# A new order for the steps of a pooled attention and feed-forward kernel, with new buffer lists

## The chip, the cores and the metric

One Trainium2 chip, one core. The metric is device time in microseconds (us); the times are medians of a few runs of the same program.

## What is computed

Attention over pooled keys and values, and a feed-forward layer whose hidden value is the largest of three products. The reference, cut to what matters:

```python
# q, k, v: (8, 8, 576, 64): batch, heads, sequence, head size
k_p = k.reshape(B, H, Sp, 8, D).mean(axis=3)      # Sp = 72
v_p = v.reshape(B, H, Sp, 8, D).mean(axis=3)
scores = (1.0 / np.sqrt(D)) * np.matmul(q, k_p.transpose(0, 1, 3, 2))
attn = np.exp(scores - scores.max(-1, keepdims=True))
attn = attn / (attn.sum(-1, keepdims=True) + 1e-09)
a = np.matmul(attn, v_p)
x = a.transpose(0, 2, 1, 3).reshape(4608, 512)
h = np.maximum(np.maximum(x @ w1, x @ w2), x @ w3)   # 512 -> 768
out = h @ w_out                                      # 768 -> 512
```

## The kernel before

**Two pipelines that run interleaved.** The attention goes by batch `b` (0 to 7, 576 tokens each), the feed-forward layer by token block `n` (0 to 8, 512 tokens each). Each engine works through its own instructions strictly in order; the order in which the Python code emits them is fixed by hand (`manual_schedule`), from two long lists of step names, `MIDDLE` and `ORDER`. A step is one piece of work with a part on TensorE (PE) and, mostly, an evacuation of its PSUM result on ScalarE (ACT) or VectorE (DVE). A name that ends in `-` emits the PE part alone, the same name with `+` later emits the evacuation, and a bare name emits both. Since every engine has its own queue, only the order within each engine counts; a `+` and a `-` of different engines that swap places in the list change nothing.

**Steps of the attention**, written `b:step` in `MIDDLE`, and without the colon for batches 6 and 7 in `ORDER`:

- `k` transposes the pooled keys (PE) and four copies put them into `kz` (ACT, DVE). The pooled keys come from GpSimd (POOL): `k5+2` are two of the four additions that fold `k` of batch 5 (lines 190 to 194), `v5+2` the same for the values; `k5<`, `v5<`, `q5<` issue the loads on POOL's queue. Such a load waits for the newest hidden product in the list and for the newest `T`.
- `T` is one DMA transpose of the whole `q` of a batch, on SyncE's (SP) queue (line 379).
- `s0`, `s3`, `s6` are the scores of three, three and two heads (line 256). Each takes both of the two `att` tiles in PSUM; ACT empties them with 4, 4 and 2 exponentials (line 261). In the second list the scores of batch 7 come in nine flat pieces.
- `v0` to `v4` multiply the exponentials with the values for 128 tokens (line 332, one `att` tile each); DVE takes the reciprocal and normalizes into `xn` (lines 340, 342).
- `x0` to `x4` bring `xn` into the transposed ring `xT`, from batch 3 on by a DMA transpose on SP's queue (line 317).

**Steps of the feed-forward layer**, written `n/step`. For `n` up to 5 the weights have `w1` subtracted, so that two products are enough:

- `h`, twelve per block: four matmuls of 512 columns into a `pw` tile (three in all, line 450); ACT writes the rectified first product (line 456), DVE the maximum with the second into `hT` (line 458).
- `a1` to `a4` and `b1` to `b4`: DVE differences of `xT` and of `hT` (line 686), which the output needs because it is computed with seven products in place of eight. They go into `tt`.
- `1` to `7`: those products, ten matmuls of 256 columns each (line 787). `1`, `6`, `5`, `3` build on one PSUM tile, so each waits until ACT has copied the one before (line 798); `2`, `4` and the later of `5` and `7` are added by DVE (line 801). Complete rows are stored by SP (line 736).
- `f` and `S`: DVE sums of weights for later blocks. `!` makes the next fold on POOL wait for the newest of the DVE steps `a`, `b`, `f`, `S`.

In `ORDER` blocks 6 to 8 get their hidden layer by seven products as well (`1a` to `7c`, line 864), `o1` to `o7` are the output products of blocks 5 and 7, `F` is a part of the output of block 6 (lines 498, 502), and `T` without a batch stands for the sums of `xT` that a block's products need.

**Buffers.** `SLOTS` says for each tile of a pool, in order of allocation, which buffer it takes. A tile's first write waits until the last user of the buffer's earlier tile is done.

The lists from which this section's steps are taken are in the function below.

Of the kernel before, what the change touches and what calls it, by code (L numbers as in the profile page):

```python
# [28 lines left out]
def kernel(  # L29
# [15 lines left out]
    B, H, S, D = q.shape  # L45
# [17 lines left out]
    PSUM = bass.MemoryType.PSUM  # L63

    SLOTS = """
        ps0.att:0120212012012 sb3.xn:0123450123450123450123450123450123540125
        psp.pw:012012012021021021021201201201201201202102010210120121021021
        psp.pw:02120120120120120101012010210210202012012012
        psp.att:010101010101010101010101010101101010101010101010101010101010
        psp.att:1010101001010101 sb3.osb:01201021021201 psq.sc:010110101010101010110101  # L70
        psq.pa:0101010100101
    """
    seats = {}
    for name in SLOTS.split():
# [5 lines left out]
    sb3 = Turns(ctx.enter_context(tc.tile_pool(name="sb3", bufs=1)), "sb3", seats, 3)  # L80
# [808 lines left out]
    def pool_step(name):  # L889
# [21 lines left out]
            held.clear()  # L911

    ORDER = """
        2a- 1a- b1 b3 1a+ o1 k7- 1b- 2a+ b2 o2- k7+ o6- v62- T 6a- o6+ s70- o5- vpool 1b+ s71- b4
        s70+ v62+ v63- 6a+ 5a- x62 s72- 7a- o2+ o5+ v63+ s71+ 6b- s73- 7a+ v64- 5a+ s75- 3a- s74-
        s72+ 4a- s73+ s75+ 6b+ s77- v64+ o3- s78- s74+ 4a+ x64 o7 s76- 2b- 1c- 2c- s77+ 2b+ 3a+
        s78+ s76+ v70- 5b- o4- x63 1c+ v70+ 2c+ 5b+ 3b- 6c- v71- x70 o4+ 3b+ 7b v71+ 1a- 6c+ 5c
        4b- o3+ 2a- 4b+ v72- 3c- v72+ F 7c- 1b- v73- T 2b- 1a+ 2a+ x71 7c+ 2c- v73+ 6a- 3c+ 1b+ 4c
        v74- 6b- 6a+ 2b+ x72 x73 5a F 3a- 7a- 2b- F 6b+ 7a+ 5b- v74+ 3a+ x74 1c 4a 5b+ F 7b- 6c-
        7b+ 2c+ 3b- F 4b- 2a- 6c+ 3b+ 1a- 5c- 4b+ 7c- 1a+ 5c+ F 7c+ 2a+ 3c- T 6a- 4c 1b- 3c+ 2c-  # L920
        6a+ 1b+ H 5a 6b- 7a- 6b+ 3a- o1- h 1c- 7a+ 5b- 3a+ 4a- o2- o1+ 1c+ 7b- 2b+ 5b+ o6- 4a+ 7b+
        6c- 4b- 2c+ o6+ o7- 6c+ 5c- 4b+ 7c- 5c+ o5- 7c+ 3c- o5+ o2+ 3b- o7+ 4c- o3- 3c+ o4- 3b+
        4c+ o3+ o4+
    """

    def weave():
# [40 lines left out]
        1/h 2:s0- 2:s0+ 2:s0+ 2:q2 1/h- 2:s0+ 1/h- 2:s0+ 1/h+ 1/b1 S 2:q3 1/h+ 1/h- S S 3:T S 1/h+  # L967
        1/a3 2:s3- 1/a1 2:s3+ 2:s3+ 1/h- 2:s3+ 1/h- 1/h+ 1/h+ 1/a2 1/h- 2:s3+ 1/a4 2:s6- 2:s6+
        1/1- 2:s6+ 1/h+ 1/b3 1/b2 1/b4 2:v0 1/2- 1/1+ 1/6- 2:v1 2:x0 1/7- 2:v2- 1/6+ 2:x1 1/5-
        1/2+ 1/7+ 2:v2+ ! k3+4 2:v3- v3+2 2:v3+ 1/5+ 2:x2 2:v4 1/3- 1/4- 2:x3 1/3+ 1/4+ 2:x4 2/h  # L970
        k5< 3:k- 2/h- 3:k+ 2/h+ 2/a1 2/a3 2/h- 2/a2 f 2/a4 f ! v3+2 v5< 2/h+ f 3:s0- 3:s0+ 3:s0+
        3:s0+ 2/h- 2/h- 2/h- 2/h+ 2/h+ 3:s0+ 2/h- 2/h+ 3:s3- 2/h+ 2/h- f 3:s3+ 2/h- 3:s3+ 2/h+
        2/h- 3:s3+ 2/b1 3:s3+ 3:s6- 2/h+ 3:s6+ 2/h- 2/h+ 2/h- 3:s6+ ! k4+2 2/h+ 2/h+ 2/b2 2/b3
        2/b4 ! k4+2 2/1- 4:T 3:v0- 2/1+ 3:v1- 3:v0+ 3:x0 2/2- 3:v1+ 2/6- 3:v2- 2/7- 3:x1 2/2+ 2/7+
        v4+2 2/6+ 3:v2+ 2/5- 3:v3- 2/5+ 3:v3+ 3:x2 3:x3 3:v4 4:k 3:x4 2/3- 2/4 2/3+ q5< 3/a3 k6<
        3/h 3/a1 3/h- 3/h- 3/h+ 3/a2 4:s0- f 3/a4 ! v4+2 4:s0+ 4:s0+ f 3/h- 3/h+ 4:s0+ 3/h+ 4:s0+
        3/h- 3/h- 3/h+ 3/h+ 4:s3- 3/h- v6< 3/h+ 3/h 4:s3+ 4:s3+ 4:s3+ 4:s3+ 3/h- 3/b1 3/h- 3/h+
        3/h+ 4:s6- 4:s6+ ! k5+2 3/h 3/h- 4:s6+ 3/1- 3/h+ 3/b2 3/b3 3/b4 3/1+ ! k5+2 v5+2 4:v0-
        3/2- 4:v0+ 4:x0 4:v1 3/6- 3/2+ 4:x1 3/6+ 3/7- 5:T 3/7+ 4:v2- 3/5- 4:v2+ ! 3/5+ 5:k- 4:v3-
        4:v4- 4:v3+ 5:k+ 4/h- 4:v4+ q6< 4/a1 4/h+ 3/3- 4/h- 4/h- 3/4- 4/a2 4/h+ 4:x2 4/h- 5:s0-  # L980
        k7< 4/a3 v5+1 f v5+1 3/4+ 4/h+ f 5:s0+ 4/h- 4:x3 4/h+ 4/h- 4/h- 5:s0+ 4:x4 5:s0+ 5:s0+
        4/h+ 4/h- 4/a4 4/h+ 5:s3- 6:T 4/h- 4/h- ! 3/3+ 4/h- 4/h+ k6+1 5:s3+ 4/h+ 4/h+ 5:s3+ 4/b1
        5:s3+ k6+1 5:s3+ 4/h+ 4/h+ 4/h 5:s6- 5:s6+ 4/b2 5:s6+ ! 4/1- 4/2- k6+1 4/b3 5:v0- k6+1
        5:v0+ 5:x0 v6+1 q7< 4/1+ 4/2+ 4/6- v6+1 5:v1- 4/6+ 5:v1+ 5:x1 4/7- 5:v2- 4/7+ 5:v2+ 4/5-
        v7< 4/b4 5:v3- 6:k- 5:v4- 4/5+ 5:v4+ 4/3- 5:v3+ 5/a3 5/h- 5/a1 6:k+ 5/h- 5:x2 6:s0- 5/h+
        6:s0+ 6:s0+ 4/4- 6:s0+ 5/h- 6:s0+ 5/h+ 6:s3- 5/h- 4/3+ 5/h- 6:s3+ 4/4+ 5:x3 5/h- 6:s6-
        5/h- ! 5/h+ 6:s3+ 5/h- 6:s3+ v6+2 k7+1 5/h+ 6:s3+ 5/a2 5/h+ 5/h- 5/h+ 6:s6+ 5/a4 5/h+
        6:s6+ 5/h- 5/h+ 5/h+ 6:v0- 5/h+ k7+1 6:v1- 5:x4 6:v0+ 6:x0 5/h- k7+1 5/h- k7+1 7:T 6:v1+
        6:x1 5/h+ 5/h+
    """  # L990
    folds = iter([f for wi in range(1, 3) for f in [fold_w(wi)] * 4])

# [85 lines left out]
```

## Time and profile before

| | |
|---|---|
| runs | 224.08, 226.4, 224.12 us; median 224.12 us |
| profiled execution | 224.31 us, of which the span of the core is 222.6 us |
| PE busy | 212.2 us (95%), 1885 matmuls |
| PE weight loads | 147.2 us (66%) |
| DVE, POOL, ACT busy | 164.0 (74%), 141.0 (63%), 122.6 us (55%) |
| granted TensorE clock | 0.997 |
| DMA | 33.55 MB, 151 GB/s in the mean |

The span runs from the first to the last instruction of the core; what lies around it is 1.7 us in this execution. PE is the engine that is almost always busy, so the time is read from PE's idle stretches and from what ended each; idle time of the other engines counts only where PE waits for them.

### The profile page before, as it was taken

What the parts mean: (1) busy time and instruction counts of PE and PEld (TensorE: products, weight loads), DVE (VectorE), ACT (ScalarE), POOL (GpSimd) and SP (SyncE); (2) the same over time, 40 slices, a digit from 0 to 9 for tenths busy, and PEclk for the clock granted to TensorE, in tenths of its full rate; (3) what the DMA queues carried; (4) which work ended last, traced back from release to release, by engine and by line L of the source; (5) the groups of instructions that cost most, each with busy time, mean ns of one, the idle gap of its engine ahead of it and who ended that gap; (6) DMA issues with size and microseconds to landing.
All of it is one profiled execution on the core that took longest, in us unless ns stands there. A gap on an engine that the chain in (4) does not pass through costs nothing.

```text
span 222.6 us, 4865 instructions
## 1 busy us (share of the span) xinstructions
PE 212.2 (95%) x1885; PEld 147.2 (66%) x1885; DVE 164.0 (74%) x308; ACT 122.6 (55%) x239; POOL 141.0 (63%) x121
## 2 busy tenths in 40 slices
PE   7798999989999999999997999999999999999992
PEld 2477744448649734974594549645899777788882
DVE  3658989037899695966487987767988988797940
ACT  2267534845784478265725673784695544553440
POOL 7974300999985969696767588995193724682020
PEclk9999999999999999999999999999999999999998
DMA  6999999989879599739986999997641574100365
GB/s 176 211 197 197 207 208 208 206 154 223 160 140 196 92 160 241 131 71 157 281 133 131 177 176 214 153 216 127 147 38 33 107 171 90 46 21 3 78 193 157
DMA packets 47303, 33.55 MB, mean 151 GB/s; under 512 B 26992, under 2 KB 42288, under 8 KB 47280
## 3 DMA queue, kind: packets, MB, share of 16 engines
q0 software_dynamic: 16944, 16.98, 47.9%
q1 hardware_dynamic: 29888, 15.87, 31.7%
q10 hardware_dynamic: 448, 0.39, 0.7%
q8 instruction: 15, 0.25, 0.4%
q14 instruction: 8, 0.07, 0.1%
HBM read 34.60 MB, written 9.44 MB: 198 GB/s over the span
## 4 chain that ended last, share of the span: by engine, by line
PE 88%; DVE 4%; DMA 3%; issue 1%; ACT 1%; SPq 0%; ACTq 0%
PE pw L450 27%; PE oA L787 14%; PE pA L864 7%; PE oC L787 7%; PE po L502 5%; PE psc L256 4%; PE pav L332 4%; PE pC L864 4%; PE oB L787 3%; PE po L498 3%; DMA ktTrue<-in_k_dram 3%; PE pm L437 2%; PE pB L864 2%; PE pqt L222 2%; PE pxt L323 2%; DVE xn L342 1%
## 5 line engine op out<-in xcount | busy, mean ns | idle before, releaser
L450 PE MATMUL pw<-xT,mw 128*128 128x512 f16 (+1 forms) x336 | 68.5, 349 | 1.7 <-issue 1.5
L450 PEld LDWEIGHTS <-mw 128*128 128x128 f16 x336 | 30.8, 98 | 27.3 <-issue 3.2
L190 POOL TENSOR_TENSOR half<-vt 72x1024 f32<-72x1024 f16 (+1 forms) x12 | 29.4, 2463 | 20.9 <-DMA vt<-in_v_dram 13.7
L261 ACT ACTIVATE et<-psc 72x512 f16<-72x512 f32 (+2 forms) x66 | 34.0, 572 | 11.1 <-PE psc L256 11.0
L458 DVE TENSOR_TENSOR hT<-t,pw 128x512 f16<-128x512 f16 (+1 forms) x42 | 25.3, 607 | 15.9 <-PE pw L450 11.0
L192 POOL TENSOR_TENSOR half<-half 72x1024 f32<-72x1024 f32 (+1 forms) x13 | 28.2, 2169 | 9.3 <-DVE tt L686 3.5
L456 ACT ACTIVATE t<-pw 128x512 f16<-128x512 f32 (+1 forms) x42 | 22.6, 538 | 17.2 <-PE pw L450 16.8
L342 DVE TENSOR_TENSOR xn<-pav,rcp 128x512 f16<-128x512 f32 x40 | 27.6, 691 | 1.4
L190 POOL TENSOR_TENSOR half<-ktFalse 96x768 f32<-96x768 f16 (+1 forms) x11 | 19.8, 1813 | 4.5 <-issue 4.3
L873 ACT CAST pad<-pA 128x512 f16<-128x512 f32 x27 | 15.5, 587 | 11.4 <-PE pA L864 11.4
L787 PEld LDWEIGHTS <-tt 128*128 128x128 f16 x200 | 18.9, 98 | 2.6 <-issue 0.2
L798 ACT COPY osb<-oA 128x512 f32<-128x512 f32 x20 | 11.8, 588 | 15.3 <-PE oA L787 15.0
L332 PE MATMUL pav<-vp,et 72*128 72x65 f16 x320 | 16.2, 194 | 0.8 <-ACT osb L507 0.7
L332 PEld LDWEIGHTS <-et 72*128 72x128 f16 x320 | 14.8, 98 | 2.5 <-issue 1.1
L841 DVE TENSOR_TENSOR pad<-pad,pC 128x512 f16<-128x512 f16 x18 | 12.3, 683 | 4.7 <-PE pC L864 3.3
L256 PEld LDWEIGHTS <-kz 64*128 64x128 bf16 (+1 forms) x161 | 8.9, 95 | 10.0 <-issue 7.4
L864 PEld LDWEIGHTS <-sw 128*128 128x128 f16 x144 | 13.6, 98 | 2.8 <-issue 0.2
L844 DVE SCALAR_TENSOR_TENSOR hT<-pad 128x512 f16<-128x512 f16 x18 | 14.5, 816 | 0.9 <-ACT pad L877 0.6
L340 DVE RECIPROCAL rcp<-pav 128x8 f32<-128x8 f32 x40 | 8.1, 202 | 9.2 <-PE pav L332 9.0
L256 PE MATMUL psc<-qT,kz 64*128 64x256 bf16 (+5 forms) x138 | 13.2, 263 | 0.8 <-DVE qT L224 0.6
L787 PEld LDWEIGHTS <-hT 128*128 128x128 f16 x126 | 12.3, 98 | 1.4
L638 POOL TENSOR_TENSOR pad<-xT 128x256 f16<-128x256 f16 x8 | 5.3, 667 | 12.3 <-DMA xT<-xn 12.3
(122 smaller groups left out, 406.4 us busy)
## 6 DMA issues: line engine op xcount, KB each, us to landing
out_dram<-osb SPq DMA_DIRECT2D x32, 128.0 KB, 4.4
ktFalse<-in_k_dram POOLq DMA_DIRECT2D x7, 576.0 KB, 8.0
qb<-in_q_dram POOLq DMA_DIRECT2D x7, 576.0 KB, 7.7
vt<-in_v_dram POOLq DMA_DIRECT2D x7, 576.0 KB, 10.6
out_dram<-osb SPq DMA_DIRECT2D x11, 256.0 KB, 5.6
mw<-in_moe_w_dram POOLq DMA_DIRECT2D x9, 256.0 KB, 9.2
ktTrue<-in_k_dram SPq DMA_DIRECT2D x3, 384.0 KB, 5.2
out_dram<-ob SPq DMA_DIRECT2D x8, 128.0 KB, 2.9
```

The lines of the kernel that those rows point to most:

```text
L190: yield e.tensor_tensor(out=f[:, at], in0=t[:, at, 0:4, :], in1=t[:, at, 4:8, :], op=ALU.add)
L192: yield e.tensor_tensor(out=f[:, :, 0:2, :], in0=f[:, :, 0:2, :], in1=f[:, :, 2:4, :], op=ALU.add)
L256: nc.tensor.matmul(out, kz_all[b % 2][f % 2][rows, h, :], qTs[b][rows, n + i0:n + i1, 64 * (h % 2):64 * (h % 2) + 64], start=True, stop=True)
L261: nc.scalar.activation(out=out, in_=in_, func=FT.Exp, scale=1.0 / 64.0)
L332: nc.tensor.matmul(pav[:, h // 4, 65 * (h % 4):65 * (h % 4) + 65], ets[b][:, h, c0:c0 + 128], vp_all[:, b, h, :], start=True, stop=True)
L342: nc.vector.tensor_tensor(out=xn, in0=pv[:, :, :, 0:D], in1=rcp.to_broadcast([128, 2, 4, D]), op=ALU.mult)
L450: mm = nc.tensor.matmul(pw, w_sb[wi][:, kc, bass.ts(jc, 128)], x[:, kc], start=(kc == 0), stop=(kc == KCH - 1))
L456: yield lambda t=t, pw=pw: nc.scalar.activation(out=t, in_=pw, func=FT.Relu)
L458: yield lambda t=t, pw=pw: nc.vector.tensor_tensor(out=hT[:, jc, c0:c1], in0=t, in1=pw, op=ALU.max)
L787: nc.tensor.matmul(p, left, right, stop=(r == 4), skip_group_check=True, start=(i in FIRST and r == 0 and (m == 0 or n == LAST)))
L864: mm = nc.tensor.matmul(p[:, w], a[:, kc, bass.ts(g, 128)], b[:, kc, :], start=(i in FIRST and w + kc == 0), stop=(w + kc == 2), skip_grou ...
L873: nc.scalar.copy(out=kept(i, g), in_=p)
```

## The change

`MIDDLE` keeps its first 170 steps, up to the middle of the seven output products of block 1 (about 73 us into the span), and gets a new order behind them; `ORDER` is new from the start. The steps are the same ones and as many. The entries of `SLOTS` change with the order of allocation, and the entry of `psq.sc` moves to the end. No function changes. Of the diff, the parts that the text speaks of (the rest of both lists is new in the same way):

```diff
-        psp.pw:02120120120120120101012010210210202012012012
+        psp.pw:01212121021021021010101021021021010101012012
...
-        1/2+ 1/7+ 2:v2+ ! k3+4 2:v3- v3+2 2:v3+ 1/5+ 2:x2 2:v4 1/3- 1/4- 2:x3 1/3+ 1/4+ 2:x4 2/h
-        k5< 3:k- 2/h- 3:k+ 2/h+ 2/a1 2/a3 2/h- 2/a2 f 2/a4 f ! v3+2 v5< 2/h+ f 3:s0- 3:s0+ 3:s0+
...
-        3/h- 3/h- 3/h+ 3/h+ 4:s3- 3/h- v6< 3/h+ 3/h 4:s3+ 4:s3+ 4:s3+ 4:s3+ 3/h- 3/b1 3/h- 3/h+
-        3/h+ 4:s6- 4:s6+ ! k5+2 3/h 3/h- 4:s6+ 3/1- 3/h+ 3/b2 3/b3 3/b4 3/1+ ! k5+2 v5+2 4:v0-
-        3/2- 4:v0+ 4:x0 4:v1 3/6- 3/2+ 4:x1 3/6+ 3/7- 5:T 3/7+ 4:v2- 3/5- 4:v2+ ! 3/5+ 5:k- 4:v3-
-        4:v4- 4:v3+ 5:k+ 4/h- 4:v4+ q6< 4/a1 4/h+ 3/3- 4/h- 4/h- 3/4- 4/a2 4/h+ 4:x2 4/h- 5:s0-
...
+        1/2+ 1/7+ ! 2:v2+ 1/5+ 2:v3 k3+1 2:v4- k3+2 2:x2 1/3- k3+1 1/4- v3+1 3:k- v3+1 2:v4+ 2/h-
+        1/3+ 3:k+ 1/4+ 2:x4 2/h- 2/h+ 2/h- 2/h+ f 2/a1 2/a3 f 3:s0- 2/a2 2/h- f k5< ! 2/h- v5<
...
+        4:s0+ 3/h- 3/h+ 4:s0+ 2/4+ 3/h- f 4:s0+ 3/h- ! 3/h- 3/h+ v4+2 4:s0+ ! 3/h+ 3/h+ 4:s3-
+        4:s3+ 4:s3+ 4:s3+ 3/a2 3/h- 3/h+ 3/h+ k5+1 4:s3+ v6< 3/a3 3/h- 3/h- 3/h+ 3/h- 3/h+ 3/h+
+        3/b1 4:s6- 4:s6+ 3/b3 3/a4 4:s6+ 3/1- 3/b2 4:v0 4:v1 3/2- 3/1+ k5+1 3/6- ! 4:v2- 3/7- 4:x1
+        3/b4 k5+2 3/2+ v5+1 3/6+ 3/5- 4:x0 4:v3- 3/7+ 4:v2+ 3/5+ 4:v3+ 4:v4- 5:k- 5:T 4:v4+ 5:k+
+        v5+1 3/3- q6< f 4/a3 4/a1 3/4- 4/h- 4/h- 5:s0- k7< 4/h- 4/h+ ! 5:s0+ 4/h- v5+1 4/h- 5:s3-
...
+        k6+1 5:s6+ 4/1- 5:s6+ 5:v0- 4/h+ 4:x4 4/b2 5:v1- 4/2- k6+1 5:v0+ ! 4/b3 k6+1 6:T 4/1+ 4/6-
+        k6+1 5:v1+ 4/7- 4/b4 5:v2- 5:x0 4/2+ 4/6+ 4/7+ 5:v2+ 4/5- 5:x1 6:k- 4/5+ v6+1 5:v3- v6+1
+        q7< 5:v4- 5:v3+ 5:v4+ 6:k+ v7< 4/3- 5/a1 4/4- 6:s0- 5/a2 6:s0+ 5/h- 5/a3 6:s0+ 5:x2 5/h-
...
+        6:v0+ 5/h+ 5/h- 5:x4 6:x0 6:v1+ 5/a4 k7+2 5/h+ 5/h- 5/h- 7:T 5/h+ 6:x1 5/h+ k7+1
```

More of the change, by code (lines that the diff above doesn't have):

```diff
@@ L65 @@
     SLOTS = """
-        ps0.att:0120212012012 sb3.xn:0123450123450123450123450123450123540125
-        psp.pw:012012012021021021021201201201201201202102010210120121021021
-        psp.pw:02120120120120120101012010210210202012012012
-        psp.att:010101010101010101010101010101101010101010101010101010101010
-        psp.att:1010101001010101 sb3.osb:01201021021201 psq.sc:010110101010101010110101
-        psq.pa:0101010100101
+        ps0.att:0120212012012 sb3.xn:0123450123450123450213450231450231450231
+        psp.pw:012012012021021021021201201201201201202102010210120212012012
+        psp.pw:01212121021021021010101021021021010101012012
+        psp.att:010101010101010101010101010101101010101010110101010101010101
+        psp.att:0101010101010101 sb3.osb:01201020120120 psq.pa:0101010100101
+        psq.sc:010101101011011011001010
     """
@@ L913 @@
     ORDER = """
[L914 to L923, printed above, removed]
+        1a- b1 1a+ b3 1b- 2a- 1b+ o1- 2a+ k7- o1+ o2- b2 o6- k7+ T 6a- o6+ 6a+ v62- vpool o2+ s70-
+        o5- s70+ s71- s72- 6b- 5a- 7a- v62+ o5+ s72+ x62 s75- b4 s71+ v63- 7a+ 5a+ s75+ s73- 3a-
+        6b+ s73+ s74- 4a- s74+ 5b- v64- 5b+ s77- s76- v63+ o7- 4a+ s76+ x63 v64+ s78- 3b- o7+ 2c-
+        1c- s77+ 3a+ 2b- s78+ v70- o4- v70+ 1c+ x64 2b+ x70 6c- o4+ o3- 2c+ 7b- 3b+ 7b+ 6c+ v71-
+        o3+ v71+ 1a- 5c- 4b T F 1a+ v72- 5c+ x71 3c- 2a- 2c- v72+ 2a+ 7c- v73- 7c+ 1b- x72 2b- 6a-
+        4c- v73+ 3c+ 1b+ 6b- v74- 6a+ 5a- x73 5a+ 4c+ F 2b+ 3a- 7a- 2b- 6b+ F v74+ 7a+ 1c- 4a- 3a+
+        4a+ 1c+ 5b- x74 5b+ F 6c- 7b- 3b- 6c+ 7b+ 3b+ F 4b- F 5c- 2c+ 1a- 7c- 5c+ T 3c- 4b+ 2a-
+        1a+ 7c+ 2a+ 6a- 4c- 1b- 3c+ 6a+ 5a- 2c- 7a- 4c+ 5a+ 3a- 7a+ H o1- 1b+ 3a+ 1c- 4a- 6b- 1c+
+        6b+ o2- 4a+ 5b- 7b- 6c- h 2b+ o1+ 5b+ o6- 7b+ 2c+ 6c+ 5c- 4b- o7- 4b+ o6+ o2+ 5c+ 7c- o5-
+        7c+ 3c- o5+ o7+ 3c+ 4c- 3b o3- 4c+ o4 o3+
     """
@@ L969 @@
         1/1- 2:s6+ 1/h+ 1/b3 1/b2 1/b4 2:v0 1/2- 1/1+ 1/6- 2:v1 2:x0 1/7- 2:v2- 1/6+ 2:x1 1/5-
-        1/2+ 1/7+ 2:v2+ ! k3+4 2:v3- v3+2 2:v3+ 1/5+ 2:x2 2:v4 1/3- 1/4- 2:x3 1/3+ 1/4+ 2:x4 2/h
-        k5< 3:k- 2/h- 3:k+ 2/h+ 2/a1 2/a3 2/h- 2/a2 f 2/a4 f ! v3+2 v5< 2/h+ f 3:s0- 3:s0+ 3:s0+
-        3:s0+ 2/h- 2/h- 2/h- 2/h+ 2/h+ 3:s0+ 2/h- 2/h+ 3:s3- 2/h+ 2/h- f 3:s3+ 2/h- 3:s3+ 2/h+
-        2/h- 3:s3+ 2/b1 3:s3+ 3:s6- 2/h+ 3:s6+ 2/h- 2/h+ 2/h- 3:s6+ ! k4+2 2/h+ 2/h+ 2/b2 2/b3
-        2/b4 ! k4+2 2/1- 4:T 3:v0- 2/1+ 3:v1- 3:v0+ 3:x0 2/2- 3:v1+ 2/6- 3:v2- 2/7- 3:x1 2/2+ 2/7+
@@ L975 @@
-        v4+2 2/6+ 3:v2+ 2/5- 3:v3- 2/5+ 3:v3+ 3:x2 3:x3 3:v4 4:k 3:x4 2/3- 2/4 2/3+ q5< 3/a3 k6<
-        3/h 3/a1 3/h- 3/h- 3/h+ 3/a2 4:s0- f 3/a4 ! v4+2 4:s0+ 4:s0+ f 3/h- 3/h+ 4:s0+ 3/h+ 4:s0+
-        3/h- 3/h- 3/h+ 3/h+ 4:s3- 3/h- v6< 3/h+ 3/h 4:s3+ 4:s3+ 4:s3+ 4:s3+ 3/h- 3/b1 3/h- 3/h+
-        3/h+ 4:s6- 4:s6+ ! k5+2 3/h 3/h- 4:s6+ 3/1- 3/h+ 3/b2 3/b3 3/b4 3/1+ ! k5+2 v5+2 4:v0-
-        3/2- 4:v0+ 4:x0 4:v1 3/6- 3/2+ 4:x1 3/6+ 3/7- 5:T 3/7+ 4:v2- 3/5- 4:v2+ ! 3/5+ 5:k- 4:v3-
-        4:v4- 4:v3+ 5:k+ 4/h- 4:v4+ q6< 4/a1 4/h+ 3/3- 4/h- 4/h- 3/4- 4/a2 4/h+ 4:x2 4/h- 5:s0-
@@ L981 @@
[L981 to L986, printed above, removed]
@@ L987 @@
-        5/h- ! 5/h+ 6:s3+ 5/h- 6:s3+ v6+2 k7+1 5/h+ 6:s3+ 5/a2 5/h+ 5/h- 5/h+ 6:s6+ 5/a4 5/h+
-        6:s6+ 5/h- 5/h+ 5/h+ 6:v0- 5/h+ k7+1 6:v1- 5:x4 6:v0+ 6:x0 5/h- k7+1 5/h- k7+1 7:T 6:v1+
-        6:x1 5/h+ 5/h+
+        1/2+ 1/7+ ! 2:v2+ 1/5+ 2:v3 k3+1 2:v4- k3+2 2:x2 1/3- k3+1 1/4- v3+1 3:k- v3+1 2:v4+ 2/h-
+        1/3+ 3:k+ 1/4+ 2:x4 2/h- 2/h+ 2/h- 2/h+ f 2/a1 2/a3 f 3:s0- 2/a2 2/h- f k5< ! 2/h- v5<
+        2/h- 3:s3- 2/h- 2/h+ v3+1 2/h- 3:s0+ 2/a4 2/h- v3+1 3:s0+ 3:s6- 2/h+ 3:s0+ ! 3:s0+ 2/h+
@@ new lines @@
+        2/h+ 3:s3+ f 3:s3+ 2/h+ 2/h+ 2/h- 3:s3+ k4+1 3:s3+ 3:s6+ 2/b1 3:s6+ 2/h- 4:T 2/h+ 3:v0-
+        2/h+ 2/h+ 3:v1- 2/h- 2/1- 2/h+ 3:v0+ 2/2- 2/1+ 3:x0 k4+1 2/b2 ! k4+1 2:x3 2/6- 2/b3 3:v1+
+        3:v2 2/2+ 2/7- k4+1 2/6+ v4+1 2/5- v4+1 3:v3- 3:x1 3:x2 2/b4 4:k- q5< k6< 3:v3+ 3:x3 3:v4-
+        2/7+ 2/5+ 3:v4+ 2/3- 3/h- 4:k+ 3:x4 3/h- 4:s0- 3/h- 3/h+ 3/h- 2/3+ 3/h+ 3/h+ 2/4- 3/a1
+        4:s0+ 3/h- 3/h+ 4:s0+ 2/4+ 3/h- f 4:s0+ 3/h- ! 3/h- 3/h+ v4+2 4:s0+ ! 3/h+ 3/h+ 4:s3-
+        4:s3+ 4:s3+ 4:s3+ 3/a2 3/h- 3/h+ 3/h+ k5+1 4:s3+ v6< 3/a3 3/h- 3/h- 3/h+ 3/h- 3/h+ 3/h+
@@ new lines @@
+        3/b1 4:s6- 4:s6+ 3/b3 3/a4 4:s6+ 3/1- 3/b2 4:v0 4:v1 3/2- 3/1+ k5+1 3/6- ! 4:v2- 3/7- 4:x1
+        3/b4 k5+2 3/2+ v5+1 3/6+ 3/5- 4:x0 4:v3- 3/7+ 4:v2+ 3/5+ 4:v3+ 4:v4- 5:k- 5:T 4:v4+ 5:k+
+        v5+1 3/3- q6< f 4/a3 4/a1 3/4- 4/h- 4/h- 5:s0- k7< 4/h- 4/h+ ! 5:s0+ 4/h- v5+1 4/h- 5:s3-
+        5:s0+ 4/h+ 4/h+ 5:s0+ v5+1 4/h- 5:s0+ 4:x2 4/h+ 4/h+ 5:s3+ f 4/h- 3/4+ 5:s3+ 4/h- 5:s3+
+        4/h- 4/h+ 4/a2 f ! 4/h- 4/h- 4/h+ 5:s3+ 3/3+ 4/a4 4/h+ 4/h+ 4/h- 4/b1 4:x3 4/h+ 4/h+ 5:s6-
+        k6+1 5:s6+ 4/1- 5:s6+ 5:v0- 4/h+ 4:x4 4/b2 5:v1- 4/2- k6+1 5:v0+ ! 4/b3 k6+1 6:T 4/1+ 4/6-
@@ L990 @@
+        k6+1 5:v1+ 4/7- 4/b4 5:v2- 5:x0 4/2+ 4/6+ 4/7+ 5:v2+ 4/5- 5:x1 6:k- 4/5+ v6+1 5:v3- v6+1
+        q7< 5:v4- 5:v3+ 5:v4+ 6:k+ v7< 4/3- 5/a1 4/4- 6:s0- 5/a2 6:s0+ 5/h- 5/a3 6:s0+ 5:x2 5/h-
+        5/h- 5/h+ 6:s0+ 6:s0+ 5/h+ 5/h+ 6:s3- 5/h- 5/h- ! 5/h+ 5/h- 6:s3+ 6:s3+ 6:s3+ 6:s3+ v6+1
+        5/h+ 6:s6- 5/h- 5/h- v6+1 5:x3 5/h+ 4/4+ k7+1 6:s6+ 6:s6+ 5/h- 4/3+ 6:v0- 6:v1- 5/h+ 5/h+
+        6:v0+ 5/h+ 5/h- 5:x4 6:x0 6:v1+ 5/a4 k7+2 5/h+ 5/h- 5/h- 7:T 5/h+ 6:x1 5/h+ k7+1
     """
```

## The prediction

> **What bounds the kernel now.** First the page, for the engines and the chain that ended last.
>
> ```profile
> PE 212.2 (95%) x1885; PEld 147.2 (66%) x1885; DVE 164.0 (74%) x308; ACT 122.6 (55%) x239; POOL 141.0 (63%) x121
> PE 88%; DVE 4%; DMA 3%; issue 1%; ACT 1%; SPq 0%; ACTq 0%
> ```
>
> PE is busy 95% of the span, and 88% of the chain is PE's own work. Then the stretch that the new order touches, from 74 us to the end of the second list at 209 us (columns: length, then busy time of each engine with its instructions), and PE's waits in it.
>
> ```profile
> 74.00:209.00 135.00, 133.30 (x1168) 94.18 (x1166) 106.93 (x188) 77.95 (x152) 90.34 (x71) 1.00 0.67 127
> ...
> PE pw L450 <- issue: 1.5, 1, 1.5
> PE psc L256 <- ACT kz L242: 0.2, 1, 0.2
> ```
>
> In these 135 us PE is idle for 1.70 us. The same work is issued in any order, so a better order can give back little more than that. 1% of the time, 2.2 us, is about what a measurement of this kernel can tell from no change. What the order can take away has no such limit. Almost all of the idle time is one wait. Last the timeline around it, on PE and on SP's queue (start, length).
>
> ```profile
> 116.64 0.68 PE L332 MATMUL pav<-vp,et 72*128 72x65 f16 x16
> 118.81 1.02 PE L450 MATMUL pw<-xT,mw 128*128 128x512 f16 x4 [1.49 <-issue]
> ```
>
> ```profile
> 113.62 1.21 SPq L317 DMA_TRANSPOSE xT<-xn  x1
> 114.94 1.21 SPq L317 DMA_TRANSPOSE xT<-xn  x1
> 116.25 2.92 SPq L379 DMA_TRANSPOSE qT<-qb  x1
> ```
>
> From issue to landing, for the second of these alone, for all 27 of line 317, and for the `T` of 116.25:
>
> ```profile
> DMA to landing us min/median/max: 3.8/3.8/3.8
> ...
> DMA to landing us min/median/max: 2.3/2.5/7.2
> ...
> DMA to landing us min/median/max: 4.9/4.9/4.9
> ```
>
> The wait is the first `4/h`. It reads the tokens of `4:x1`, issued at 114.94; that one lands after 3.8 us, at 118.7, where the median of all 27 is 2.5. Right behind it SP issues `5:T`, which lands after 4.9 (the lowest of the five `T` is 4.0).
>
> **What the change does to it.** PE's list is the same steps; I price each place where the new neighbours make PE wait, or stop making it wait. Prices of PE steps are the spacing of their starts: `h` 0.86, an output product 1.09, `v` 0.26, `s0`/`s3` 0.49, `s6` 0.38, `k` 0.13.
>
> (1) *The wait at 117.3 goes*: −1.49. Behind `4:v1` PE had 4.2 us of work before `4/h`, and the first `4/h` came ahead of `3/3`. Now `3/2`, `3/3` and `3/4` lie between as well. Bounds: −1.49, and 0 if the transposes come later by as much (5).
>
> (2) *`3:s0` no longer waits for the key copies*: −0.33. Its first score matmul starts 0.47 us ahead of the second, for 0.13 us of columns (320 at the rate of four `h` matmuls of 512 in 0.86): 0.33 lost, 0.15 of it idle. `3:k` moves ahead of the first `2/h`: three `h` and a transpose, 2.8 us, lie between it and `3:s0`, where the copies need 1.0 once ACT is free. Bounds −0.33 and 0.
>
> (3) *`4:v0` and `5:v0` come too soon behind the scores*: +0.34. They read the last exponentials of `s6`:
>
> ```profile
> 87.28 1.18 ACT L261 ACTIVATE et<-psc 72x512 f16<-72x512 f32 x2 [0.59 <-PE psc L256]
> ```
>
> `s6` starts at 86.86, the exponentials end at 88.46: 1.60 us. Before, two `h` or a second product lay between; now `s6` 0.38 and one product 1.09, together 1.47. With 0.04 of signalling, 0.17 each. Bounds 0 and 0.7 (an `h` copy of 0.6 ahead of them on ACT).
>
> (4) *`3/6` waits for `3/b2` on DVE*: +0.70. Let the last `3/h` end at 0. PE: `s6` 0.38, `3/1` 1.47, wait of (3) to 1.64, `v0` and `v1` 2.16, `3/2` 3.25, then `3/6`, which needs `b2`. DVE, by the spacing in the block before (0.45 to 0.48 behind each other): maximum at 0.27, `b1` 0.99, `b3` 1.47, `a4` 1.95, `b2` 2.3 to 2.85: in time, if nothing holds it. But a DVE step with both inputs in SBUF that meets a fold on POOL stands until the fold ends:
>
> ```profile
> 125.45 2.67 DVE L686 TENSOR_TENSOR tt<-xT,tt 128x512 f16<-128x512 f16 x1
> 129.37 2.02 DVE L686 TENSOR_TENSOR tt<-hT 128x768 f16<-128x768 f16 x1
> ...
> 125.46 2.37 POOL L192 TENSOR_TENSOR half<-half 72x1024 f32<-72x1024 f32 x1
> 129.33 3.55 POOL L190 TENSOR_TENSOR half<-ktFalse 96x768 f32<-96x768 f16 x2
> ```
>
> These took 2.67 and 2.02 us where their medians are 0.42 and 0.55, ending 0.3 and 0.4 behind the fold (127.83; the first of the two folds of the last line at 130.97). In the new list the third fold of `v4` is gated by an `f` some 1.5 us behind `2/4`, which ends at −7.4 (eight `h`, one score step). From −5.9 POOL does folds of 2.5, 1.3 and 1.6 and the issue of `v6`, 0.9: its next fold, 1.63 long, runs from 0.4 to 2.05. `b1`, wanted at 0.99, starts at 2.05; `b2` ends at 3.9; `3/6` starts at 3.95 in place of 3.25. Bounds 0 (POOL 1.1 us earlier or later) and 1.6 (the whole fold).
>
> (5) *`5:T` is late for `5:s0`*: +1.0. Behind (4), `4:v1`'s `xn` ends at 5.6. SP issues `4:x1`, `4:x0`, `5:T` 1.3 apart: 5.6, 6.9, 8.2. PE: `3/6` 3.95, `v2` 5.04, `3/7` 5.30, `3/5` 6.39, `v3`, `v4`, `5:k` to 8.1, `3/3` 8.15, `3/4` 9.24, `4/h` 10.33, `5:s0` 12.06. `x0` lands at 9.4 to 10.7, `T` at 12.2 (by 4.0) to 13.1 (by 4.9). PE waits 0.1 to 1.0 in all. I take 1.0: two `x` and a `T` in a row are just what landed in 4.9 before. The ends are 0.1 and 1.0; with a load in flight an `x` took up to 7.2, which is in a rival below.
>
> (6) *`6:s0` follows `4/4` directly*: +0.25. It needs the `att` tile that `5:v4` leaves. From the end of `4/5`: the copy and the addition end at 1.27, two pairs of reciprocal and normalization (0.84, then 0.93) at 3.05; PE has `k`, two `v`, and from 0.67 on `4/3` and `4/4`: 2.85. Before, two `h` stood there too. Bounds 0 and 2 (`b4` of block 4, in the same queue, behind a fold of 2.1).
>
> *At nothing:* the rest of both lists. `6:x0` and `7:T`: from `6:v0` to the first score of batch 7 PE has 8.5 us (it had 7.7), the way over `xn`, `x0` and `T` took 7.1 (152.60 to 159.68). Without that cover each us is one of PE. The load of `v5` now follows `k5` at once, 5 us earlier, beside the stores of block 1 and `4:T` on the other queue; `4:T` is hidden by some 17 us of PE work up to `4:s0`, but `3:x0` to `3:x2` queue behind it, with 2.8 us between the last of them and `3/h` (the 3.3 of before, 94.92 to 98.23, less `2/4`, plus an addition that now follows on DVE); it needs 2.5. `v6` goes 2 us later behind a fold, and is wanted 20 us later. The second list changes neighbours by a product or two, and each product's copy is 0.59 against products of 0.44 to 1.09 behind it, as before.
>
> Sum: −1.49 − 0.33 + 0.34 + 0.70 + 1.0 + 0.25 = +0.47 us. On the profiled execution's 224.31 that is 224.8; it lies 0.19 above the median of the runs, 224.12, so I say **224.6 us**: no change that can be measured.
>
> **A rule beside the row of (4).** The Trainium skill (SBUF — State Buffer, "Who interferes with whom") says that a DVE instruction with two SBUF inputs and a GpSimd instruction that reads SBUF exclude each other for the whole instruction, and that whoever starts first holds the ports. The two rows above agree. If the ports were shared instead, `b1` would be slowed in part and (4) would be near 0; by the rule the price is what is left of the fold. By the same rule the new order, which spreads these DVE steps between the folds, could lose more than I sum, and that is the second rival.
>
> **Rivals.**
> *The gain stays.* POOL misses `b1` and `T` lands in 4.0: (4) is 0, and from (5) at most 0.1 to 0.3 is left. −1.82 + 0.34 + 0.25 + 0.2 = −1.03: 223.1. For it: 2.3 to 2.5 is the usual landing, and the meeting of (4) hangs on 1 us. Against it: the list does put `T` behind two `x`. If (3) and (6) vanish too: 222.3, hardly 1%.
>
> *DVE falls behind between the folds: slower.* Place: blocks 2 to 4. Before, the `b` steps of a block stand together ahead of a gated fold; the new list has `2/b4`, `3/a2`, `3/a3`, `3/b1`, `4/b4` alone among maxima and normalizations while POOL folds. Price: the rest of a fold, 0.76, 2.25 and 1.47 us in three rows before, mean 1.5. The rows are 1.31, 2.67 and 2.02 us in place of 0.55, 0.42 and 0.55. They reached PE nowhere, because DVE (107 us busy of 135) had slack behind them. It decides from the point where the delay is larger than the PE work up to the next use of the `pw` or `att` tile, about 2 `h`, 1.7 us: two meetings in one block. Two more meetings that reach PE: 224.6 + 3.0 = 227.6; one: 226.1. For it: five places against three. Against it: half of the meetings fall where nothing waits.
>
> *The transposes run into the loads: slower.* `x` landed after 6 to 7.2 us four times, each with a load in flight. If `3:x2` or `4:x0` meets one, `3/h` or `4/h` waits some 3 us: 227.6; if `T` alone, 1 to 2: 226.
>
> **How the numbers follow.** The forecast 0.50 (224.6, own range 223.6 to 225.8), the gain stays 0.21 (222.3 to 223.6), DVE behind the folds 0.20 (225.8 to 228), transposes in the loads 0.09 (225.5 to 228). Faster by over 1% (below 221.9): 0.03, the end of the second case with the small waits of 0.15 to 0.2 us behind copies gone as well. Slower by over 1% (above 226.4): three quarters of the third, two thirds of the fourth and 0.03 of the first: 0.24. The rest, 0.73, lies between. The range is 222.6 to 227.2: it cuts half of the last two cases' upper parts and the tip of the second.
>
> **What would show it.** Right: the 1.5 us ahead of the first `4/h` gone; 0.2 ahead of `4:v0` and `5:v0`; `3/6` behind a `b2` that ends late, its `b1` over 1 us long; `5:s0` started by the landing of `5:T`. PE idle from 74 us to the end of the second list between 1.5 and 3 us. Wrong: several DVE rows of line 686 above 1.5 us with PE waiting for `pw` or `att`; an `x` that lands after 5 us or more right ahead of an `h`; or PE idle below 0.8 us.

## The result and the profile after

The changed kernel takes **240.5 us** in the median (239.1 to 245.3), the kernel before on the same chip 224.5; the ratio is 1.067 [1.058, 1.077]. The forecast was 224.6 with a range up to 227.2. The profiled execution takes 239.1 us, its span is 237.3. Some executions of a kernel show a lower granted clock and take longer; the ratios leave these out.

The page's rows for the engines and for the chain that ended last:

```profile
PE 213.6 (90%) x1885; PEld 147.4 (62%) x1885; DVE 160.9 (68%) x308; ACT 123.2 (52%) x239; POOL 141.9 (60%) x121
PE 65%; DMA 18%; POOL 7%; DVE 3%; SPq 3%; issue 2%; POOLq 0%; DVEq 0%
```

PE does the same work (213.6 us busy, 212.2 before), but it is 90% of the span in place of 95%, and DMA now holds 18% of the chain, 3% before. That share says little by itself: e11 below has 16% of it without the loss. The stretch from 74 us to the end of the second list, now near 224 us, cut in four (length, then busy time of PE, PEld, DVE, ACT, POOL with instructions, granted clock, DMA share, GB/s), and PE's waits in it:

```profile
74.00:90.00 16.00, 16.00 (x121) 8.82 (x119) 13.18 (x25) 10.23 (x21) 13.94 (x10) 1.00 1.12 141
90.00:112.00 22.00, 8.89 (x87) 6.62 (x85) 6.60 (x14) 4.33 (x9) 8.99 (x7) 0.74 1.30 89
112.00:124.00 12.00, 12.00 (x66) 5.68 (x65) 6.64 (x10) 6.71 (x15) 6.99 (x5) 0.91 0.72 164
124.00:224.00 100.00, 98.78 (x902) 73.79 (x901) 78.36 (x141) 57.65 (x109) 61.40 (x51) 1.00 0.56 112
```

```profile
PE pw L450 <- DMA xT<-xn: 13.1, 1, 13.1
PE psf L256 <- DMA qT<-qb: 0.8, 1, 0.8
PE psc L256 <- DMA qT<-qb: 0.4, 1, 0.4
```

Nearly all of the loss is in the second row: 22 us with 8.89 of PE work. One wait makes it, 13.1 us, ended by a transpose of `xn`. PE's timeline there, and that of SP's queue:

```profile
96.00 0.82 PE L787 MATMUL oA<-so,hT 128*128 128x256 f16 x6
109.92 3.57 PE L450 MATMUL pw<-xT,mw 128*128 128x512 f16 x8 [13.09 <-DMA xT<-xn]
```

```profile
80.08 5.71 SPq L379 DMA_TRANSPOSE qT<-qb  x1
90.62 18.05 SPq L317 DMA_TRANSPOSE xT<-xn  x6
```

The step that waits is the first `3/h`; the six transposes are those of batch 3, whose first three steps it reads, all behind `4:T` on SP's queue. The DMA issues of this moment, with KB and microseconds from issue to landing, first of the kernel before, then of the changed one:

```profile
ktFalse<-in_k_dram POOLq DMA_DIRECT2D x1, 576.0 KB, 6.7
vt<-in_v_dram POOLq DMA_DIRECT2D x1, 576.0 KB, 8.3
...
qT<-qb SPq DMA_TRANSPOSE x1, 10.1
```

```profile
ktFalse<-in_k_dram POOLq DMA_DIRECT2D x1, 576.0 KB, 25.5
vt<-in_v_dram POOLq DMA_DIRECT2D x1, 576.0 KB, 27.2
...
qT<-qb SPq DMA_TRANSPOSE x1, 27.5
```

The same three transfers, k5 (`ktFalse`), v5 (`vt`) and `4:T` (`qT`), take 25 to 28 us in place of 7 to 10. Before, k5 was issued at 79.51 and `T` at 82.07; now `T` comes first, at 80.08, and k5 0.67 us behind it, at 80.75. The bytes hardly move: in the second row the packets under way add up to a share of 1.30 of the 16 DMA engines' time, for 89 GB/s.

The wait costs more than its length. After it, eight `h` matmuls start 427 ns apart in place of 216, at a granted clock of 0.51 from 109.9 to 114.2. With the scores behind them they take 4.3 us for what takes 2.3 in e11 below: 2.0 us lost. Then 239.1 − 13.1 − 2.0 = 224.0 us, an estimate for the changed kernel without this one meeting of transfers. That it lies near the forecast is partly luck, as the other steps below show.

### The profile page after: what moved, and what is told of

Read it like the earlier page. It is cut to its first block, busy times and chain, and to the rows that moved or that the text cites. A ratio compares the mean times of both kernels' runs of the same rounds, so it can differ in the third digit from the quotient of the medians.

```text
span 237.3 us, 4877 instructions
## 1 busy us (share of the span) xinstructions
PE 213.6 (90%) x1885; PEld 147.4 (62%) x1885; DVE 160.9 (68%) x308; ACT 123.2 (52%) x239; POOL 141.9 (60%) x121
## 4 chain that ended last, share of the span: by engine, by line
PE 65%; DMA 18%; POOL 7%; DVE 3%; SPq 3%; issue 2%; POOLq 0%; DVEq 0%
PE pw L450 22%; PE oA L787 10%; DMA vt<-in_v_dram 8%; PE pA L864 6%; PE oC L787 6%; DMA mw<-in_moe_w_dram 4%; DMA xT<-xn 3%; DMA qT<-qb 3%; PE pC L864 3%; PE psc L256 3%; PE pav L332 3%; SPq L317 3%; PE po L502 3%; PE oB L787 2%; PE po L498 2%; POOL half L190 2%
## 5 line engine op out<-in xcount | busy, mean ns | idle before, releaser
L450 PE MATMUL pw<-xT,mw 128*128 128x512 f16 (+1 forms) x336 | 70.1, 355 | 13.3 <-DMA xT<-xn 13.1
L190 POOL TENSOR_TENSOR half<-vt 72x1024 f32<-72x1024 f16 (+1 forms) x12 | 29.9, 2511 | 20.3 <-DMA vt<-in_v_dram 13.2
L261 ACT ACTIVATE et<-psc 72x512 f16<-72x512 f32 (+2 forms) x66 | 33.9, 569 | 10.7 <-PE psc L256 10.6
L192 POOL TENSOR_TENSOR half<-half 72x1024 f32<-72x1024 f32 (+1 forms) x13 | 27.8, 2140 | 10.6 <-DVE tt L686 7.7
L873 ACT CAST pad<-pA 128x512 f16<-128x512 f32 x27 | 15.4, 586 | 10.1 <-PE pA L864 8.7
L126 POOL DMA_DIRECT2D qb<-in_q_dram x9 | 7.1, 784 | 13.9 <-DMA qT<-qb 11.7
L638 POOL TENSOR_TENSOR pad<-xT 128x256 f16<-128x256 f16 x8 | 6.3, 794 | 12.6 <-DMA xT<-xn 12.6
L844 DVE SCALAR_TENSOR_TENSOR hT<-pad 128x512 f16<-128x512 f16 x18 | 13.1, 727 | 0.9 <-ACT pad L877 0.6
```

The source lines that it names most:

```text
L190: yield e.tensor_tensor(out=f[:, at], in0=t[:, at, 0:4, :], in1=t[:, at, 4:8, :], op=ALU.add)
L192: yield e.tensor_tensor(out=f[:, :, 0:2, :], in0=f[:, :, 0:2, :], in1=f[:, :, 2:4, :], op=ALU.add)
L261: nc.scalar.activation(out=out, in_=in_, func=FT.Exp, scale=1.0 / 64.0)
L450: mm = nc.tensor.matmul(pw, w_sb[wi][:, kc, bass.ts(jc, 128)], x[:, kc], start=(kc == 0), stop=(kc == KCH - 1))
L873: nc.scalar.copy(out=kept(i, g), in_=p)
```

## The experiments

In e1, e2 and e9 `4:T` also leaves its old place in the list; the diffs show the places it moves to. Three theories. **A**: `4:T` and the loads slow each other down while they are in flight together, and the rest follows from SP's order. **B**: two loads in flight together are slow by themselves. **C**: the loss lies in PE's order. Ratios are against the kernel before on the same chip. To crawl means here that a transfer of 576 KB takes over 15 us.

**e1: the loads wait for T.**

```diff
-        ... 2/a2 2/h- f k5< ! 2/h- v5<
+        ... 2/a2 2/h- f 4:T k5< ! 2/h- v5<
```

> Theory A: 4:T (a DMA transpose on SP's queue) and the loads of k5 and v5 (GpSimd's queue) slow each other down while they are in flight together: T landed after 27.5 us, the loads after 25.5 and 27.2, and the x transposes of block 3 behind T on SP's queue came 13.1 us late for 3/h. Here 4:T is listed ahead of both loads, so they wait for its landing; SP's order is as before. A expects T to land after 4 to 6 us, the loads after 7 to 10, no wait of PE ahead of the first 3/h, no matmuls at half rate behind it, and 239.1 - 13.1 - 1.8 = 224.2 us, between 223.4 and 225.2. Theory B: the two loads are slow because they are issued within 1.2 us of each other (before, 6.5 us lay between), and T only stood behind them: the loads still take over 20 us here, T alone lands early, and as nothing of block 3 waits for k5 or v5 the time is near 224 too; the landings tell A from B. Theory C: the loss lies in the order of PE's steps and not in the transfers: 237 us or more.

Measured: `T` 4.8 us, k5 6.3, v5 8.8, with the loads issued 0.5 us apart. That ends B: two loads together are not slow. There is no wait ahead of `3/h`, which ends C. The time is 228.2 us, profile 226.93, ratio 1.010 [1.001, 1.020], more than I expected by one wait:

```profile
PE pav L332 <- POOL vp L194: 3.6, 2, 3.0
```

POOL stood at k5's load from 79.5 to 85.25, until `T` had landed, and the folds of the values behind it came 3.0 us late for PE. Without it the profile is at 223.9. Two of the four runs take 229.4 and 229.6 us, at a granted clock of 0.982 in place of 1.000; no trace shows where they lost it.

**e2: the meeting brought about in the kernel before**, with `4:T` between the two groups of stores and k5 not gated (`k5<<`).

```diff
-        ... 2:x3 1/3+ 1/4+ 2:x4 2/h
-        k5< 3:k- ...
+        ... 2:x3 1/3+ 4:T 1/4+ 2:x4 2/h
+        k5<< 3:k- ...
```

> The kernel before, with 4:T issued on SP's queue between the two groups of block 1's stores (near 79.9 us instead of 82.1), and k5's load no longer waiting for the newest h or T, so that the two are in flight together; v5's load stays behind T's landing. A expects T and k5 both to land after more than 12 us (before: 10.1 and 6.7), v5 to follow late, the x transposes of block 2's end and block 3 behind T on SP's queue to land late, and a time of 226 to 240 us with a wait of PE for xT. B (two loads together are needed) expects T to land after 4 to 10 us, k5 after 7, and 224 to 225 us.

Measured: k5 (issued at 79.66, 0.43 us **ahead** of `T`) 7.4 us, `T` 10.6, v5 7.8. A as I had put it is wrong: the two were in flight together and nothing crawled. The trace's packets say why: k5's moved from 81.5 to 86.2, `T`'s from 85.8. The time, 229.5 us, ratio 1.016 [1.007, 1.026], comes from something else: v5's load waited for `T` (landed at 90.7, v5 issued at 91.3), POOL behind it, and PE lost 2.4 us to a fold of the keys and more to the clock, which was 0.66 from 98 to 103 us.

**e3 and e4: one load alone at its place**, the other behind two folds of v3.

```diff
 e3  ... f k5< ! 2/h-                 ... 2/a4 2/h- v3+1 v5< 3:s0+
 e4  ... f ! 2/h- v5<                 ... 2/a4 2/h- v3+1 k5< 3:s0+
```

> The changed kernel with v5's load alone moved some 6 us later on GpSimd's queue, behind two folds; k5's load and 4:T stay where they are and meet alone. A, if one load is enough: T and k5 both land after 12 us or more (half of the bytes, so about half of the 25 to 27 us), and PE waits up to 3 us ahead of 3/h: 225 to 230 us; v5, gated only on what is listed ahead of it, may join them and bring it back to 235 to 240. B: k5 lands after 7 us, T within 10, no wait: 224 us.

> As the one before, with k5's load moved behind the two folds and v5's load at its early place: 4:T meets v5 alone. A: the same as there, 225 to 240 us, with T and v5 landing late; if the size or the layout of k5's packets made the difference, only one of the two shows it. B: T within 10 us, v5 after 8, no wait: 224 us.

Landings of k5, v5 and `T` in e3:

```profile
ktFalse<-in_k_dram POOLq DMA_DIRECT2D x1, 576.0 KB, 26.9
vt<-in_v_dram POOLq DMA_DIRECT2D x1, 576.0 KB, 24.4
qT<-qb SPq DMA_TRANSPOSE x1, 28.4
```

e3 is the changed kernel again: 240.5 us, 1.065 [1.054, 1.076], 14.8 us ahead of `3/h`; one load less at the start did not shorten it, and v5 joined later. e4 has none of it, against what A expected: v5 7.6 us, k5 7.5, `T` 7.7, and 223.7 us, 0.991 [0.982, 0.9995]. So k5's early load is what counts. Either k5's packets are the bad ones (6144 bytes, v5's have 1024), or the moment: in e4 v5 was issued 1.8 us behind `T`, and its packets began at 84.3, when `T`'s (82.2 to 84.5) were nearly through.

**e5, e6, e7: packets or moment?** e5 puts v5's load at exactly k5's place (and k5 where e4 has it), e6 loads k5 in six parts of 1024 bytes a partition, e7 issues k5 ungated, ahead of `T`.

```diff
 e5  ... f v5< ! 2/h-                 ... v3+1 k5< 3:s0+
 e6  +        parts = 6 if b == 5 else parts        (load_k)
 e7  -  ... f k5< ! 2/h- v5<
     +  ... f k5<< ! 2/h- v5<
```

> The kernel of e4 with v5's load at exactly the place that k5's load has in the changed kernel (issued near 80.8 us instead of 82.1), so that its first packets come near 82.8, in the middle of T's (82.1 to 84.4 where nothing disturbs them). In e4 they came at 84.0, when 0.4 us of T was left. If any load whose packets join T's under way makes both crawl, T and v5 land after over 20 us and the time is 237 to 242 us. If it takes k5's packets of 6144 bytes (v5's have 1024), T lands within 10 us, v5 after 7 to 9, and the time is that of e4, 223.0 to 224.4.

> The changed kernel with k5's load issued in six parts of 1024 bytes a partition in place of one of 6144; the place and the bytes are the same. GpSimd needs 5 x 0.55 = 2.75 us more to issue them, so the folds of v3 end later and PE may wait 2 to 3 us for them near 87 us. If the size of k5's packets makes the crawl, T lands within 10 us, there is no wait of 13 us ahead of 3/h, and the time is 224 to 228 us. If any load that joins T under way does it, T lands after over 15 us and the time is over 234.

> The changed kernel, with k5's load at the same place of the list but not held until the newest h: it is issued when GpSimd is free, near 79.6 us, 1.1 us sooner, and ahead of T (80.1) instead of 0.67 us behind it. The kernels in which k5 was issued first (before, e2) show T's packets waiting until the last of k5's had gone. Theory A in its sharper form, that the crawl needs T's packets first and k5's joining them: no crawl, k5 lands after 7 us, T after 9 to 11, no wait at 3/h, 223.4 to 224.6 us. If being in flight together is enough: T over 20 us, and 237 or more.

e5: `T` 8.1, v5 8.3, 224.1 us, 0.993 [0.986, 0.9999]. It decides nothing: v5's first packets came 3.2 us after the issue, at 84.2, so the meeting did not take place. e6: the parts land after 3.6 to 8.6 us, `T` after 10.6, PE waits nowhere for it; 223.6 and 226.6 us, 0.997 [0.989, 1.006]. The packets of both did mix here, at a mild price. But the place is not that of the changed kernel: `load_k` returns only its last part, so the wait for the newest `h` holds that one alone, and the first part was issued at 79.06, ahead of `T` at 79.57. So e6 changes the order together with the size and decides nothing between them. e7 missed, and tells most:

```profile
ktFalse<-in_k_dram POOLq DMA_DIRECT2D x1, 576.0 KB, 7.0
vt<-in_v_dram POOLq DMA_DIRECT2D x1, 576.0 KB, 16.0
...
qT<-qb SPq DMA_TRANSPOSE x1, 18.0
```

k5 went first, unharmed, and `T` waited as expected. But so held back, `T` was under way when v5's packets came, at 86.2, and these two, with packets of 256 and of 1024 bytes, now slowed each other to 18 and 16 us, and `3/h` waited 2.7. The profile is of a run at 227.7 us, and another took 228.0; the ratio, 0.996 [0.988, 1.004], rests on the other two, at 223.6 and 225.9, of which no trace shows whether the two met. So this one trace shows that it does not take k5's packets, but a load that joins while `T`'s packets are moving. How many are left when the load's first packets come parts all these traces: 1437, 1513 and 1737 of `T`'s 2304 where it crawled (e3, the changed kernel, e7), 114 and 55 where it did not (e4, e5).

**e11: the moment alone.** k5 behind one more `2/h`, 1 us later, v5 directly behind it.

```diff
-        ... f k5< ! 2/h- v5<
+        ... f ! 2/h- k5< v5<
```

> The changed kernel with k5's load moved behind one 2/h in the list, so that it is issued some 1.2 us later, near 81.9, with v5 directly behind it (82.5). Its first packets then come at about 84, when T's (82.1 to 84.4 undisturbed) are nearly through. If the moment at which the packets join decides, T lands within 10 us, k5 and v5 after 8 to 12, and the time is 223.5 to 225. If it is enough that T has not landed when the loads are issued, T, k5 and v5 take over 15 us and the time is 233 to 242.

```profile
ktFalse<-in_k_dram POOLq DMA_DIRECT2D x1, 576.0 KB, 7.3
vt<-in_v_dram POOLq DMA_DIRECT2D x1, 576.0 KB, 11.5
...
qT<-qb SPq DMA_TRANSPOSE x1, 8.6
```

k5 is issued at 81.71, its first packets come at 84.3, with 58 of `T`'s left, and nothing crawls: **223.75 us** (223.3 to 224.7 in eight runs), 0.996 [0.992, 0.999]. Swapping two neighbours in the list is worth 16 us, by the two ratios. The rates (last column, GB/s) of the stretches in which `T` and loads move, in e11, in the changed kernel, and in e7 from v5's first packets on:

```profile
82.00:88.00 6.00, 6.00 (x50) 2.91 (x49) 5.95 (x8) 4.37 (x10) 5.82 (x5) 1.00 1.10 207
```

```profile
83.00:106.00 23.00, 13.80 (x135) 9.77 (x133) 12.31 (x22) 8.47 (x17) 14.51 (x8) 0.88 1.31 70
```

```profile
86.00:96.00 10.00, 9.98 (x116) 8.23 (x114) 7.76 (x16) 4.78 (x10) 8.76 (x6) 1.00 1.47 114
```

One behind the other they move at 207 GB/s, mixed at 70 or 114. In e11 `T` alone goes at 288 GB/s from 83 to 84 us, and k5 alone at 184 from 85 to 86.

**e10: is it the transpose?**

```diff
-                turned[:] = [nc.sync.dma_start_transpose(
+                turned[:] = [nc.sync.dma_start(
+                    out=qTs[b].rearrange("p a c -> p (a c)"),
+                    in_=qbs[b].rearrange("p hp t d -> p (hp t d)")) if b == 4 else
+                    nc.sync.dma_start_transpose(
```

> The changed kernel, with 4:T alone turned from a transpose into a plain copy of the same tile and bytes by the same queue at the same place (what it leaves out is the transposition of block 4's queries). k5 is issued as before it in the changed kernel. If the slow stretch needs the transpose, the copy lands after 3 to 8 us, k5 after 7 to 9, v5 after 8 to 10, no 13 us ahead of 3/h: 223.6 to 224.6 us. If any transfer on SP's queue that k5's packets join slows down so, the copy takes over 15 us and the time is 235 or more.

The copy lands after 4.2 us, k5, issued 0.68 us behind it as in the changed kernel, after 7.2, v5 after 10.8; no wait at `3/h`; 223.3 us, 0.993 [0.988, 0.998]. But the two hardly met. The queues' packets (number, MB, share of the 16 engines) from 83.5 to 84.0 in e10, then from 83.0 to 83.5 in the changed kernel, where `q0` carries k5, and `q1` the copy or `T`:

```profile
q0 software_dynamic: 11, 0.07, 121.2%
q1 hardware_dynamic: 12, 0.00, 1.3%
```

```profile
q0 software_dynamic: 6, 0.04, 148.5%
q1 hardware_dynamic: 325, 0.08, 123.5%
```

The copy's 128 packets of 4608 bytes start from 81.8 to 83.5, and k5's first comes at 83.3, when ten of them are left; in the changed kernel 1513 of `T`'s 2304 were. So e10 shows that a copy in `T`'s place is out of the way in time. Whether a copy that a load meets halfway would crawl too, and so whether the transposition or its packets of 256 bytes are needed, it leaves open.

**e8 and e9: versions that might beat both.** e8 is e4 with `5:T` ahead of `4:v0`. e9 has both loads behind the two folds of v3, gated on `4:T`.

```diff
 e8  -  3/b2 4:v0 4:v1 3/2-  ...  4:v4- 5:k- 5:T 4:v4+
     +  3/b2 5:T 4:v0 4:v1 3/2-  ...  4:v4- 5:k- 4:v4+
 e9  +  ... 2/a4 2/h- v3+1 4:T k5< v5< 3:s0+
```

> A version that may beat both: the kernel of e4, with 5:T listed ahead of 4:v0 instead of behind 5:k, so that it is no longer behind 4:x1 and 4:x0 on SP's queue. The 0.4 us of PE ahead of 5:s0 should go, and nothing else change: 223.1 us if the profile is like e4's (223.56), 0.4 to 0.7% below the kernel before on the same chip. If the rest of e4's distance to before was the chip, the ratio comes out at 0.998 to 1.000.

> A version that may beat both: the changed kernel with both loads behind the two folds of v3 on GpSimd's queue (so the folds do not wait as they did in e1, where PE lost 3.0 us to them), and with 4:T listed directly ahead of the loads, so that none can join T under way. Expected: T alone lands after 4 to 5 us, near 85; k5 and v5 are issued at 84.5 to 87 and land 7 to 9 us later; no wait for the folds and none ahead of 3/h above 0.3 us; the small waits at 5:s0 (0.4) and at the first scores of batch 7 (0.5 to 1.0) stay. 223.6 to 224.2 us by the profile of e4, and more even from run to run than the kernel before, 0.3 to 0.9% below it on the same chip. Should the gate hold GpSimd beyond 87 us, the next folds come late and the time is 225 to 227.

e8 gained nothing: 224.67 us in the run that was profiled, 229.6 to 234.2 in the other five, of which there is no trace; no ratio is on record. In the profile `5:T` is issued at 107.54 beside v6's load of 107.30 and takes 11.9 us, v6 9.2 (in e4 `5:T` was issued at 117.46, when v6 had landed, and took 4.0); `4:x1` and `4:x0` come late behind it, and the first `4/h` waits 1.5 us. I had moved another `T` into another load. That the higher runs are this meeting at its worse is argued only. e9: `T` 4.8 us, k5 5.9, v5 9.0; 224.9 us, ratio 1.000 [0.997, 1.003], where I had expected 0.3 to 0.9% less than before. Here v5 is in flight until 95.97, `3:x0` lands after 5.8 us, and `3/h` waits 0.6. Of the versions that compute the same, e4, e5 and e11 lie 0.4 to 0.9% below the kernel before, and all three intervals nearly touch 1; e4 and e5 have two runs each, e11 eight.

## Why the prediction was wrong

**The step that failed** is in the part priced at nothing: "The load of `v5` now follows `k5` at once, 5 us earlier, beside the stores of block 1 and `4:T` on the other queue; `4:T` is hidden by some 17 us of PE work up to `4:s0`, but `3:x0` to `3:x2` queue behind it [...] it needs 2.5." It saw the place, the two queues and the steps behind. It took for granted that `T` and the loads keep their durations. It also looked at v5, and not at k5 and `T`, whose order on the two queues was what the change turned round: 2.56 us ahead before, 0.67 us behind now. The trace of before had a hint that I passed over: this `T` took 10.1 us and the one of 129.79 took 8.3, where the other three took 4.0 to 4.9. The packets of both waited until a load's packets of 6144 bytes had gone (k5's, for `4:T`), and v5's began at 89.0, when those of `4:T` ended. The old order kept three transfers apart by chance, within a fraction of a microsecond.

**The rival of transposes that run into the loads** (0.09) had the right mechanism at the right step, `3/h` behind `3:x2`. Its size was wrong: 3 us, from an `x` that landed after 7 us beside a load, for 13.1 and 2.0. An `x` of line 317 that meets a load is one thing; a whole `T` of 576 KB that meets one took over 20 us longer, and six `x` queued behind it. No row of before showed such a meeting, so its upper bound should have been open.

A rule bears on this. The Trainium skill (DMA: Bandwidth & Descriptors, "Rules for kernel authors") says that a transpose next to ordinary DMAs needs nothing, unlike two transposes from different queues, which corrupt each other's data. Read as advice on the time, the traces here contradict it: 27.5 us against 4.8 for the same `T`.

**The other steps** are read where nothing stalls, in e11. PE's waits there from 74 to 209 us:

```profile
PE psc L256 <- DMA qT<-qb: 0.4, 1, 0.4
PE psf L256 <- DMA qT<-qb: 0.3, 1, 0.3
```

(1) The wait at the first `4/h` is gone, in e11 and in the changed kernel: −1.49, right. (2) `3:s0` starts without the loss of 0.33: right. (3) No wait ahead of `4:v0` and `5:v0`: 0 for +0.34. (4) `b1` is not held: 0 for +0.70. In e11 the fold of 1.65 us that I put behind the end of the last `3/h` ended 0.3 us after it, 1.7 sooner than I had it, and the next began only when the normalization released it, after `b2`. I had given this step the bound 0, but had taken the middle. (5) `5:T` is late for `5:s0` by 0.45 (0.38 in the changed kernel), within its 0.1 to 1.0, not the 1.0 that I took. (6) 0 for +0.25. And one that stood at nothing: the first scores of batch 7 wait 0.3 for `7:T` (0.8 in the changed kernel). Sum for e11: −1.49 − 0.33 + 0.45 + 0.3 = −1.1 us; the ratio of 0.996 is −0.9 (−0.2 to −1.7). So among the kernels without the meeting the first rival, "the gain stays" at 223.1, was nearer than the forecast: I had added up four small waits, of which three came to nothing and one to half.

## What to carry to other kernels

A step list that moves DMAs on two queues can change which of them is in flight beside which; list for each pair the issue times, the first and last packets, and what stands behind it on its queue, before calling a transfer hidden. A large DMA transpose and a load should follow each other: put the load ahead by its whole length, with no second load that joins the transpose (e7), or behind the transpose's packets, by the order of the list, and look at the wait that a gate would put on the work behind it (POOL's folds lost 2.4 to 3.0 us to one). Where a transfer meets one that it never met in the trace, its price has no upper bound from that trace, and the range should say so.

## What the hardware showed that I had not expected

**The meeting.** `T` and a load in mixed flight moved 70 to 114 GB/s together, against 288 and 184 alone, and both landed after 16 to 28 us in three kernels. A second load issued 0.5 us behind the first, a load that came with 114 or fewer of `T`'s packets left, or a `T` whose packets waited until the load's had gone, or all but 4 of 96 (the kernel before, e2), brought no such thing. In the changed kernel the packets themselves took longer: k5's of 6144 bytes 1.2 us in the mean and up to 6.8, against 0.6 in e1, and those of 256 bytes on SP's queue 0.1 in the mean and up to 1.9, against 0.018. A load in packets of 1024 bytes fared better than one of 6144, in one trace each (e7, 114 GB/s, against 70). What in the DMA engines does it, and whether it needs a transpose, is open.

**Half clock after an idle stretch.** Granted clock over the stretches behind PE's wait (third column from the end): 13.1 us in the changed kernel, 2.7 in e7, 3.0 in e1:

```profile
109.90:114.20 4.30, 4.28 (x15) 1.48 (x15) 0.61 (x2) 1.07 (x2) 0.00 (x0) 0.51 1.17 190
```

```profile
99.00:103.00 4.00, 4.00 (x16) 1.33 (x17) 0.39 (x1) 1.07 (x2) 0.51 (x1) 0.57 0.97 129
```

```profile
90.00:92.00 2.00, 1.59 (x22) 1.10 (x22) 0.00 (x0) 0.00 (x0) 1.92 (x2) 1.00 1.00 159
```

So a wait of about 3 us may cost another 1.7 us, or nothing. The Trainium skill (TensorE: Matmul & The Clock Gate, "What's actually happening") tells of a free-running window of some 3.4 us, idle in which the clock is halved. That the shorter wait lost the clock here and the longer one kept it agrees with a window that is not tied to the wait's start. But 2.7 us is less than a whole window, and here the measurement decides: so short a wait was enough.
